# A fused scan and bilinear feed-forward kernel: one sum moved to another PSUM bank, a reciprocal and several copies, masks and scalings put in another order

## The chip, the cores and the metric

The kernel runs on one core of one Trainium2 chip. A core has five engines that follow their own instruction streams and wait for each other on semaphores: TensorE (PE, matrix products, with weight loads shown as PEld), VectorE (DVE), ScalarE (ACT), GpSimd (POOL) and SyncE (SP, which here only issues DMAs). The metric is device time in microseconds (us) for one execution, taken as the median of several runs. Before the change it is 124.18 us, with single runs of 123.66, 124.18 and 124.46 us.

## The reference

A chunked state-space scan over 4 batches, 8 heads, 768 tokens, head size 32 and state size 16 is followed by a bilinear feed-forward layer over the 3072 tokens of width 256, with an inner width of 1536.

```python
# per chunk of tokens: x (b,h,q,32), a (b,h,q), B and C (b,h,q,16)
cum = np.cumsum(log_a_chunk, axis=-1)
L = np.exp(cum[..., :, None] - cum[..., None, :]) * causal
M = np.einsum('bhin,bhjn->bhij', Cc, Bc) * L
y_intra = np.einsum('bhij,bhjd->bhid', M, xc)
y_inter = np.einsum('bhin,bhnd->bhid', Cc, state) * np.exp(cum)[..., None]
y[:, :, sl] = y_intra + y_inter
Bx = np.einsum('bhjn,bhjd->bhjnd', Bc, xc) * np.exp(cum[..., -1:] - cum)[..., None, None]
state = np.exp(log_a_chunk.sum(-1))[..., None, None] * state + Bx.sum(axis=2)
...
x = y.transpose(0, 2, 1, 3).reshape(4 * 768, 256)
return ((x @ w_a) * (x @ w_b)) @ w_out
```

## The kernel before

**Tiling.** The 768 tokens of a batch are six blocks of 128 tokens. Two batches of one block form a *pair*, so there are twelve pairs; pairs 2k and 2k+1 belong to block k. For each pair the kernel scales B and C by decay factors (`bm`, `cm`, fp16), turns them with TensorE (`transposes`), forms the products of C and B (`scores`), multiplies these by the causal mask (`mask`), and multiplies the masked products by x, adding the part that comes from the state (`pv` for pairs 0 to 3, `outputs` for whole blocks from block 2 on). The result goes into the feed-forward part.

**Feed-forward.** For pairs 0 to 3 the work is cut into *units* (`unit(p, k2)`, six to a pair): four matmuls with `Wa` into one PSUM bank (the A sum), a copy of that bank to SBUF by ACT (`evac_a`, tile `asb`, line 714), four matmuls with `Wb` into another bank (the B sum), and a product of the B sum with `asb` on DVE (`times`, tile `hk`, line 721). From block 2 on, *block units* (`bunit(blk, k)`, twelve to a block) do the same with two matmuls of 512 columns to a sum (line 768, product `hkb` at line 778). `out_half` and `bout` then multiply `hk` or `hkb` by `Wo` into a bank (`ops`), which ACT copies out and SP stores.

**PSUM.** Eight banks of 512 fp32 columns are used. Four of them are the *score banks* SC[0] to SC[3], held by two tiles of two banks each (SC0 and SC1): scores, transposes of pairs 0 to 3, state sums and outputs are written there. The other four are handed out by `bank(name)` to every A sum, B sum, `ops` sum and to some transposes. Which of the four a request gets is written out by hand: the string `BANKS` has one digit for each request in program order. A matmul that starts a sum in a bank waits until the tile that had this bank last has been read.

**Masks.** The score bank m of a pair holds four heads' products. `mask(product(p, m))` reads it on DVE, multiplies by the causal tile and writes `t1` (line 497). With `by_pool=True` ACT copies the bank to SBUF first (`tmp`, line 494), and POOL multiplies (line 495), as POOL works on SBUF here.

**Order.** The program is scheduled by hand: each engine's instructions run in the order in which the Python code emits them. `masked(p, ms, *units)` emits, turn by turn, the matmuls and the ACT copy of one unit, then one DVE mask, then the product of the unit. `go` and `bgo` emit whole units, `prep(p)` the POOL scalings of B and C of pair p (line 379, or line 191 for a block's tile `mq` that DVE turns later, line 202), `prep_x(p)` the POOL scaling of x (line 368), `loads_x(p)` a DMA from POOL's queue. `over_mid` is a reciprocal on DVE (line 282, tile `rmid`); `rmid` is read by the POOL products at lines 908 and 910, which lead to the factors G, and by `late_rows` (line 321).

**Weights.** The halves `Wa[0]`, `Wb[0]` serve units 0 to 2 of a pair, `Wa[1]`, `Wb[1]` units 3 to 5. All are loaded once, from POOL's DMA queue (line 213). Inputs of pairs 3 and up are loaded from SP's queue, whose issue starts when the first half of `Wo` has landed.

Of the kernel before, what the change touches and what calls it, by code (L numbers as in the profile page):

```python
# [19 lines left out]
YS = 16.0  # L20

BANKS = (
    "0123102031203132031023102310213021302130213021302130210312031201320132031023120310213203"
    "1203120312013021320312032130123012301231032103201320132013201320132013201320132013201320"
    "13201"
)


# [1 line left out]
def kernel(  # L30
# [18 lines left out]
    NBLK = S // Q  # L49
# [38 lines left out]
    Wa = [big.tile([128, 2, KC], f16, name=f"Wa{t}") for t in range(2)]  # L88
    Wb = [big.tile([128, 2, KC], f16, name=f"Wb{t}") for t in range(2)]
# [39 lines left out]
    SC = [SC0[:, 0], SC0[:, 1], SC1[:, 0], SC1[:, 1]]  # L129
# [8 lines left out]
    def bank(name):  # L138
        return psf.tile([128, 512], f32, name=name, tag=f"ff{next(banks)}")


    def by_block(blk, which):
        return blk >= NBLK - NT and (which == 1 or blk == NBLK - 1)
# [71 lines left out]
    def w_up(W, k, f):  # L215
        t, g = k // 6, k // 3 % 2
        return W[t][:, f, g * 384 : (g + 1) * 384].rearrange("p (c kk) -> p kk c", kk=3)[:, k % 3]
# [63 lines left out]
    def over_mid(lo, hi):  # L281
        nc.vector.reciprocal(rmid[:, lo:hi], Pr[:, lo:hi, 63])
# [154 lines left out]
    def scores(p):  # L437
        BT, CT = st[p]["BT"], st[p]["CT"]
        st[p]["T1"] = mid.tile([128, H, 2, Q], f16, name="t1", tag="t1")
        for e, bt, m in itertools.product(range(2), range(2), range(4)) if p >= P0 else ():  # L440
            rows = slice(32 * m, 32 * m + 32)
            c0 = (e * 2 + bt) * Q
            nc.tensor.matmul(  # L443
                SC[m][:, c0 : c0 + Q],
                BT[rows, e, bt],
                CT[rows, bt],
                start=True,
                stop=True,
                skip_group_check=True,
                tile_position=(32 * m, 0),  # L450
            )
        for e in range(2) if p < P0 else ():
            for r in range(2):
                for m in range(4):
                    for bt in range(2):
                        rows = slice(32 * m, 32 * m + 32)
                        c0 = (e * 2 + r) * Q
                        nc.tensor.matmul(  # L458
                            SC[m][64 * bt : 64 * bt + 64, c0 : c0 + Q],
                            BT[rows, e, r, bt],  # L460
                            CT[rows, bt],
                            start=True,
                            stop=True,
                            skip_group_check=True,
                            tile_position=(32 * m, 64 * bt),
                        )

    def product(p, m):

        if p >= P0:  # L470
            return (
                st[p]["T1"][:, 2 * m : 2 * m + 2].rearrange("p e t q -> p (e t) q"),
                SC[m].rearrange("p (c q) -> p c q", q=Q),
                causal_q.unsqueeze(1).broadcast_to((128, 4, Q)),
            )
        return (
            st[p]["T1"][:, 2 * m : 2 * m + 2].rearrange("p e r q -> p e (r q)"),
            SC[m].rearrange("p (e c) -> p e c", e=2),
            causal.rearrange("p r q -> p (r q)").unsqueeze(1).broadcast_to((128, 2, 2 * Q)),
        )  # L480
# [9 lines left out]
    def mask(out_in, by_pool=False):  # L490
        o_, i_, c_ = out_in
        if by_pool:
            tmp = mid.tile([128, *c_.shape[1:]], f32, name="tmp", tag="tmp")
            nc.scalar.copy(tmp, i_)  # L494
            nc.gpsimd.tensor_tensor(out=o_, in0=tmp, in1=c_, op=ALU.mult)  # L495
        else:
            nc.vector.tensor_tensor(out=o_, in0=i_, in1=c_, op=ALU.mult)  # L497
# [184 lines left out]
            )  # L682
        st.setdefault(("S", p + NBP), {})["Sbd"] = Sbd

    def unit_mm(p, k2, W):
        ps = bank("aps" if W is Wa else "bps")
        for kk in range(2):
            k = 2 * k2 + kk
            for f in range(2):
                nc.tensor.matmul(  # L690
                    ps[:, kk * 2 * Q : (kk + 1) * 2 * Q],
                    w_up(W, k, f),
                    X2T[:, p, :, f],
                    start=(f == 0),
                    stop=(f == 1),
                    skip_group_check=True,
                )
        return ps
# [13 lines left out]
    def evac_a(a_ps, on_dve=False):  # L712
        asb = ffh.tile([128, 512], f32, name="asb", tag="asb", bufs=5)
        (nc.vector.tensor_copy if on_dve else nc.scalar.copy)(asb, a_ps)  # L714
        return asb

    def times(p, k2, b_ps, asb):
        s = st[p]
        if "hk" not in s:
            s["hk"] = ffh.tile([128, NK, 2 * Q], f16, name="hk", tag="hk")  # L720
        nc.vector.tensor_tensor(  # L721
            out=s["hk"][:, 2 * k2 : 2 * k2 + 2, :].rearrange("p k q -> p (k q)"), in0=b_ps, in1=asb, op=ALU.mult
        )

    def unit(p, k2, between=None):
        a_ps = unit_mm(p, k2, Wa)
        asb = evac_a(a_ps)
        if between:
            between()
        b_ps = unit_mm(p, k2, Wb)  # L730
        return lambda: times(p, k2, b_ps, asb)

    def out_mm(p, bt, o_ps, ks):
        hk = st[p]["hk"]
        for k in ks:
            nc.tensor.matmul(  # L736
                o_ps[:, 0:d_model],
                hk[:, k, bt * Q : (bt + 1) * Q],
                Wo[:, k, :],
                start=(k == 0),  # L740
                stop=(k == NK - 1),
                skip_group_check=True,
            )

    def out_store(p, bt, o_ps):
        blk, bp = divmod(p, NBP)
        o_sb = outp.tile([128, d_model], f32, name="osb", tag="osb")
        nc.scalar.activation(out=o_sb, in_=o_ps[:, 0:d_model], func=AF.Copy, scale=1.0 / (YS * YS))
        r0 = (2 * bp + bt) * S + blk * Q
        stores.append(lambda: nc.sync.dma_start(out[r0 : r0 + Q, :], o_sb))  # L750
        if p > 1:
            store_all()

    def out_half(p, bt):
        o_ps = bank("ops")
        out_mm(p, bt, o_ps, range(NK))
        out_store(p, bt, o_ps)
# [22 lines left out]
    def bgo(blk, *ks):  # L780
        for k in ks:
            bunit(blk, k)()
# [48 lines left out]
    def go(*items):  # L831
        for p, k2 in items:
            unit(p, k2)()
# [49 lines left out]
    aps = [bank("aps") for _ in range(3)]  # L883
# [15 lines left out]
    bps = [bank("bps") for _ in range(3)]  # L899
# [3 lines left out]
    units_mm(0, range(3), Wb, bps, 0, range(4, 6))  # L903
    units_mm(0, range(3), Wb, bps, 1, range(2, 6))
    nc.scalar.copy(maskbd, headm.unsqueeze(2).broadcast_to((128, H, D)))
    times(0, 0, bps[0], asb[0])
    over_mid(2, NBLK)
    nc.gpsimd.tensor_tensor(out=hr, in0=Pr[:, 0:NG, Q - 1], in1=rmid[:, 0:NG], op=ALU.mult)
    nc.gpsimd.tensor_tensor(out=hs, in0=hr, in1=Pr[:, 1:NBLK, 63], op=ALU.mult)
    nc.gpsimd.tensor_tensor(  # L910
# [10 lines left out]
    scale_bc(2, 0, nc.gpsimd)  # L921
    scale_bc(2, 1, nc.gpsimd)
    load_wo(1)
    go((1, 0), (1, 1))
    late_rows(nc.vector)
    rows = store_rows(nc.sync)
    go((1, 2))
# [15 lines left out]
    aps = [unit_mm(0, 3, Wa), unit_mm(0, 4, Wa)]  # L943
# [11 lines left out]
    h = unit(1, 4)  # L955
# [5 lines left out]
    h = unit(1, 5)  # L961
# [17 lines left out]
    h = unit(2, 0, lambda: transposes(3, apart=True))  # L979
    h()  # L980
    h = unit(2, 1)

    def prep(p, spread=()):
        if p < NP:
            for w in (1, 0):
                if not by_block(p // NBP, w):
                    scale_bc(p, w, nc.gpsimd)
                elif p % NBP == 0:
                    scale_block(p // NBP, w, nc.gpsimd)
        for q in spread:  # L990
            if q // NBP < NBLK - 1:
                state_spread(q)

    def prep_x(p):
        if p < NP:
            scale_x(p, nc.gpsimd)
# [17 lines left out]
    def masked(p, ms, *units):  # L1014
        for i in range(max(len(ms), len(units))):
            h = units[i]() if i < len(units) else None
            if i < len(ms):
                mask(product(p, ms[i]))
            if h:
                h()  # L1020

    def pu(p, *ks):
        return [lambda k=k: unit(p, k) for k in ks]

    def bu(blk, *ks):
        return [lambda k=k: bunit(blk, k) for k in ks]
# [26 lines left out]
    prep_x(4)  # L1053

    scores(4)
    mask(product(4, 3), by_pool=True)
    prep_x(5)
    prep(6)
    masked(4, (0, 1))
    masked(4, (2,), *pu(3, 0))  # L1060
    go((3, 1), (3, 2))
    scores(5)
    mask(product(5, 3), by_pool=True)
    out_half(2, 1)
    prep(7)
    h = unit(3, 3)
    mask(product(5, 0))
# [2 lines left out]
    h = unit(3, 4)  # L1070
# [22 lines left out]
    for p in range(9, NP):  # L1093
        loads_x(p)
    prep(10)
    masked(7, (0, 1, 2), *bu(2, 5, 6, 7, 8, 9, 10, 11))
    turn_pair(8, 1)
    group(3)
    transposes(8)
# [81 lines left out]
```

## Time and profile before

| | us |
|---|---|
| median of the runs | 124.18 |
| lowest and highest run | 123.66, 124.46 |
| the profiled execution's own time | 123.89 |
| its span (first to last instruction) | 122.2 |
| TensorE busy | 116.0 |
| VectorE busy | 92.8 |
| ScalarE busy | 76.6 |
| GpSimd busy | 65.6 |

The times inside the profile are counted from the start of the span. A row of the timeline gives the start, the busy time, the engine, the line of the kernel, the operation, the written and read tiles, the shapes and how many instructions in a row are merged into it; in brackets stands the idle time of the engine ahead of it, and who ended the idle time. Matmuls are pipelined: a row of four matmuls is shown as 0.60 us long, although the next four start 0.44 us after it. For TensorE the distance between starts is therefore the thing to read, and not the busy time. Instructions of DVE and ACT overlap in the same way by some hundredths of a microsecond.

### The profile page before, as it was taken

What the parts mean: (1) busy time and instruction counts of PE and PEld (TensorE: products, weight loads), DVE (VectorE), ACT (ScalarE), POOL (GpSimd) and SP (SyncE); (2) the same over time, 40 slices, a digit from 0 to 9 for tenths busy, and PEclk for the clock granted to TensorE, in tenths of its full rate; (3) what the DMA queues carried; (4) which work ended last, traced back from release to release, by engine and by line L of the source; (5) the groups of instructions that cost most, each with busy time, mean ns of one, the idle gap of its engine ahead of it and who ended that gap; (6) DMA issues with size and microseconds to landing.
All of it is one profiled execution on the core that took longest, in us unless ns stands there. A gap on an engine that the chain in (4) does not pass through costs nothing.

```text
span 122.2 us, 3719 instructions
## 1 busy us (share of the span) xinstructions
PE 116.0 (95%) x1440; PEld 79.1 (65%) x1440; DVE 92.8 (76%) x183; ACT 76.6 (63%) x157; POOL 65.6 (54%) x92
## 2 busy tenths in 40 slices
PE   6789799999999999999999999999999999999990
PEld 2245589889898798744467464766464775555890
DVE  4999789895886979699995999996898444847200
ACT  0447856837669855987659757666757736557220
POOL 7987997599892995083999379319034000000000
PEclk9999999999999999999999999999999999999999
DMA  3999979997996288169636991011101012010132
GB/s 67 181 161 213 207 160 218 133 179 76 110 124 117 43 82 130 37 80 126 121 73 135 253 348 60 0 48 46 43 0 43 5 43 86 0 43 5 41 88 86
DMA packets 46017, 12.25 MB, mean 100 GB/s; under 512 B 40000, under 2 KB 45568, under 8 KB 46000
## 3 DMA queue, kind: packets, MB, share of 16 engines
q1 hardware_dynamic: 41344, 7.62, 32.6%
q0 software_dynamic: 2384, 3.98, 17.2%
q10 hardware_dynamic: 2272, 0.43, 1.8%
q8 instruction: 11, 0.18, 0.6%
q14 instruction: 6, 0.05, 0.1%
HBM read 11.18 MB, written 3.19 MB: 118 GB/s over the span
## 4 chain that ended last, share of the span: by engine, by line
PE 85%; DMA 6%; POOL 4%; ACT 1%; DVE 1%; issue 1%
PE ops L793 18%; PE aps L768 17%; PE bps L768 16%; PE ops L736 9%; PE aps L690 8%; PE bps L690 7%; DMA Wb<-in_moe_w_b_dram 6%; PE SC L443 2%; PE SC L503 2%; PE bps L703 1%; POOL bn L165 1%; POOL cn L165 1%; ACT asb L714 1%; PE tr L409 1%; PE SC L518 1%; PE SC L593 1%
## 5 line engine op out<-in xcount | busy, mean ns | idle before, releaser
L714 ACT COPY asb<-aps 128x512 f32<-128x512 f32 x72 | 42.0, 589 | 14.4 <-PE aps L768 9.3
L778 DVE TENSOR_TENSOR hkb<-bps,asb 128x512 f16<-128x512 f32 x48 | 32.0, 687 | 10.5 <-ACT asb L714 9.9
L768 PE MATMUL aps<-XB,Wa 128*128 128x512 f16 x96 | 28.6, 379 | 0.1
L768 PE MATMUL bps<-XB,Wb 128*128 128x512 f16 x96 | 28.5, 379 | 0.0
L793 PE MATMUL ops<-Wo,hkb 128*128 128x256 f16 (+1 forms) x204 | 22.6, 267 | 0.0
L793 PEld LDWEIGHTS <-hkb 128*128 128x128 f16 x204 | 18.5, 98 | 3.0
L721 DVE TENSOR_TENSOR hk<-bps,asb 128x512 f16<-128x512 f32 x24 | 15.9, 683 | 3.0 <-ACT asb L714 2.1
L497 DVE TENSOR_TENSOR t<-SC,causal_q 128x512 f16<-128x512 f32 x24 | 15.5, 682 | 3.2 <-PE SC L443 3.2
L495 POOL TENSOR_TENSOR t<-tmp,causal_q 128x512 f16<-128x512 f32 x8 | 9.3, 1158 | 14.5 <-ACT tmp L494 14.3
L768 PEld LDWEIGHTS <-Wb 128*128 128x128 f16 x96 | 9.9, 103 | 10.9
L768 PEld LDWEIGHTS <-Wa 128*128 128x128 f16 x96 | 9.7, 103 | 9.2 <-issue 0.3
L368 POOL TENSOR_SCALAR x<-xn 128x512 f16<-128x512 f32 x8 | 11.9, 1492 | 3.0 <-DMA xn<-in_x_dram 2.4
L805 ACT ACTIVATE osb<-ops 128x256 f32<-128x256 f32 (+1 forms) x16 | 6.0, 378 | 11.2 <-PE ops L793 11.2
L690 PE MATMUL aps<-X2T,Wa 128*128 128x256 f16 x84 | 12.5, 273 | 0.3 <-ACT asb L714 0.2
L690 PE MATMUL bps<-X2T,Wb 128*128 128x256 f16 x84 | 12.4, 272 | 0.0
L736 PE MATMUL ops<-Wo,hk 128*128 128x256 f16 x96 | 11.6, 273 | 0.0
L736 PEld LDWEIGHTS <-hk 128*128 128x128 f16 x96 | 9.0, 98 | 1.2
L690 PEld LDWEIGHTS <-Wa 128*128 128x128 f16 x84 | 8.3, 104 | 1.3 <-issue 0.6
L690 PEld LDWEIGHTS <-Wb 128*128 128x128 f16 x84 | 8.6, 103 | 0.5
L497 DVE TENSOR_TENSOR t<-SC,causal 128x512 f16<-128x512 f32 x13 | 8.2, 682 | 0.9 <-PE SC L458 0.8
L494 ACT COPY tmp<-SC 128x512 f32<-128x512 f32 x11 | 6.6, 596 | 1.9 <-PE SC L443 1.1
L202 DVE STREAM_TRANSPOSE tq<-mq 128x256 f16<-128x256 f16 x8 | 5.9, 742 | 0.0
(111 smaller groups left out, 136.9 us busy)
## 6 DMA issues: line engine op xcount, KB each, us to landing
out_dram<-osb SPq DMA_DIRECT2D x17, 128.0 KB, 3.2
xn<-in_x_dram SPq DMA_DIRECT2D x5, 256.0 KB, 4.6
out_dram<-osb SPq DMA_DIRECT2D x13, 64.0 KB, 1.5
Wo<-in_moe_w_out_dram POOLq DMA_DIRECT2D x2, 384.0 KB, 5.0
bn<-in_B_dram SPq DMA_DIRECT2D x6, 128.0 KB, 4.0
rq<-in_C_dram SPq DMA_DIRECT2D x24, 32.0 KB, 2.2
xn<-in_x_dram POOLq DMA_DIRECT2D x3, 256.0 KB, 5.0
xn<-in_x_dram SPq DMA_DIRECT2D x4, 128.0 KB, 5.4
```

What stands on the lines that cost most here:

```text
L368: eng.tensor_scalar(xo, xi, XS, None, ALU.mult)
L494: nc.scalar.copy(tmp, i_)
L495: nc.gpsimd.tensor_tensor(out=o_, in0=tmp, in1=c_, op=ALU.mult)
L497: nc.vector.tensor_tensor(out=o_, in0=i_, in1=c_, op=ALU.mult)
L690: nc.tensor.matmul(ps[:, kk * 2 * Q : (kk + 1) * 2 * Q], w_up(W, k, f), X2T[:, p, :, f], start=(f == 0), stop=(f == 1), skip_group_check=True,
L714: (nc.vector.tensor_copy if on_dve else nc.scalar.copy)(asb, a_ps)
L721: nc.vector.tensor_tensor(out=s["hk"][:, 2 * k2 : 2 * k2 + 2, :].rearrange("p k q -> p (k q)"), in0=b_ps, in1=asb, op=ALU.mult)
L736: nc.tensor.matmul(o_ps[:, 0:d_model], hk[:, k, bt * Q : (bt + 1) * Q], Wo[:, k, :], start=(k == 0), stop=(k == NK - 1), skip_group_check= ...
L768: nc.tensor.matmul(t_, w_up(W, k, f), XB[:, blk - P0 // NBP, f].rearrange("p t j q -> p (t j q)"), start=(f == 0), stop=(f == 1), skip_gro ...
L778: return lambda: nc.vector.tensor_tensor(out=s["hk"][:, k], in0=ps[1], in1=asb, op=ALU.mult)
L793: nc.tensor.matmul(o_ps[:, 0:w], hk[:, k, c * Q : (c + 1) * Q], Wo[:, k, cs], start=(k == 0), stop=(k == NK - 1), skip_group_check=True,)
L805: nc.scalar.activation(out=o_sb[:, 0:w], in_=o_ps[:, 0:w], func=AF.Copy, scale=1.0 / (YS * YS))
```

## The change

One string is written anew, and the order of some instructions is changed. No instruction is added or removed, and TensorE's own order stays as it was.

- `over_mid(2, NBLK)` is emitted ahead of the first product of unit (0,0), and not behind it.
- The A sum of unit (1,1) goes into the score bank SC[0] instead of one of the four rotating banks. `BANKS` has one digit less, and its digits behind that place are assigned anew.
- Pairs 4 and 5: the x of pair 5 is scaled by POOL ahead of the POOL mask of pair 4 instead of behind it. The ACT copy for this mask is emitted behind ACT's copy of the A sum of unit (3,0) instead of ahead of it. The DVE mask of bank 2 of pair 4 comes behind the product of unit (3,0) instead of ahead of it. `prep(6)`, the scalings of pair 6 with the C of block 3, moves from ahead of these masks to behind the POOL mask of pair 5.
- Pair 7: its DVE mask of bank 2 moves by one unit, from the turn of block unit 7 into that of block unit 8.

```diff
 BANKS = (
-    "0123102031203132031023102310213021302130213021302130210312031201320132031023120310213203"
-    "1203120312013021320312032130123012301231032103201320132013201320132013201320132013201320"
-    "13201"
+    "0123102031203123012301230123102310231023102310231023102130213012301230210321302103123021"
+    "0321032103123012032103201231023102310213201320312031203120312031203120312031203120312031"
+    "2031"
 )
...
-    def unit_mm(p, k2, W):
-        ps = bank("aps" if W is Wa else "bps")
+    def unit_mm(p, k2, W, ps=None):
+        if ps is None:
+            ps = bank("aps" if W is Wa else "bps")
...
-    def unit(p, k2, between=None):
-        a_ps = unit_mm(p, k2, Wa)
+    def unit(p, k2, between=None, ps=(None, None)):
+        a_ps = unit_mm(p, k2, Wa, ps[0])
         asb = evac_a(a_ps)
         if between:
             between()
-        b_ps = unit_mm(p, k2, Wb)
+        b_ps = unit_mm(p, k2, Wb, ps[1])
         return lambda: times(p, k2, b_ps, asb)
...
+    over_mid(2, NBLK)
     times(0, 0, bps[0], asb[0])
-    over_mid(2, NBLK)
...
-    go((1, 0), (1, 1))
+    go((1, 0))
+    unit(1, 1, ps=(SC[0], None))()
     late_rows(nc.vector)
...
     scores(4)
+    prep_x(5)
+    masked(4, (0, 1))
+    h = unit(3, 0)
     mask(product(4, 3), by_pool=True)
-    prep_x(5)
-    prep(6)
-    masked(4, (0, 1))
-    masked(4, (2,), *pu(3, 0))
+    h()
+    mask(product(4, 2))
     go((3, 1), (3, 2))
     scores(5)
     mask(product(5, 3), by_pool=True)
     out_half(2, 1)
+    prep(6)
     prep(7)
...
     prep(10)
-    masked(7, (0, 1, 2), *bu(2, 5, 6, 7, 8, 9, 10, 11))
+    masked(7, (0, 1), *bu(2, 5, 6))
+    bgo(2, 7)
+    masked(7, (2,), *bu(2, 8, 9, 10, 11))
```

## The prediction, made before the changed kernel was run

> **What bounds the kernel now.** I read the page's busy shares and its chain of work first, then TensorE's timeline for places where the distance between starts is longer than elsewhere, and at each such place the timelines of ACT, DVE and POOL.
>
> ```profile
> PE 116.0 (95%) x1440; PEld 79.1 (65%) x1440; DVE 92.8 (76%) x183; ACT 76.6 (63%) x157; POOL 65.6 (54%) x92
> PE 85%; DMA 6%; POOL 4%; ACT 1%; DVE 1%; issue 1%
> ```
>
> TensorE is busy for 95% of the span, and 85% of the chain that ended last is TensorE's. The rest of the chain is the load of the first weights at the start. From then on the end moves only by what TensorE gains or loses between two of its own instructions, and a gap that closes is worth its length unless a later instruction then waits. Three such gaps lie where the change acts.
>
> ```profile
> 14.90 0.60 PE L690 MATMUL aps<-X2T,Wa 128*128 128x256 f16 x4
> 15.34 0.60 PE L690 MATMUL bps<-X2T,Wb 128*128 128x256 f16 x4
> 16.17 0.60 PE L690 MATMUL aps<-X2T,Wa 128*128 128x256 f16 x4 [0.24 <-ACT asb L714]
> ...
> 40.71 0.60 PE L690 MATMUL bps<-X2T,Wb 128*128 128x256 f16 x4
> 41.33 0.60 PE L690 MATMUL aps<-X2T,Wa 128*128 128x256 f16 x4
> 41.82 0.60 PE L690 MATMUL bps<-X2T,Wb 128*128 128x256 f16 x4
> 42.34 0.40 PE L443 MATMUL SC<-ct,bt 32*128 32x128 f16 x16
> ...
> 59.66 0.59 PE L768 MATMUL bps<-XB,Wb 128*128 128x512 f16 x2
> 60.32 0.59 PE L768 MATMUL aps<-XB,Wa 128*128 128x512 f16 x2
> ```
>
> A sum of four matmuls is followed after 0.44 us (14.90 to 15.34); two wide ones stream as many columns. Against that, the A sum of unit (1,1) comes 0.83 after its forerunner (15.34 to 16.17): 0.39 lost. The sums of unit (3,2) come after 0.62 and 0.49: 0.18 and 0.05, together 0.23 lost. The A sum of block unit (2,10) comes after 0.66: 0.22 lost. In all 0.84 us, the most that the change can gain here.
>
> **The change part by part.**
>
> *The A sum of unit (1,1) in SC[0].*
>
> ```profile
> 15.54 0.59 ACT L714 COPY asb<-aps 128x512 f32<-128x512 f32 x1 [0.47 <-PE aps L690]
> 16.80 0.59 ACT L714 COPY asb<-aps 128x512 f32<-128x512 f32 x1 [0.68 <-PE aps L690]
> 17.91 0.30 PE L929 MATMUL SC<-hsx,c 128*128 128x20 f32 x2
> ...
> 19.27 1.04 PE L690 MATMUL bps<-X2T,Wb 128*128 128x256 f16 x8
> ...
> L213 POOL DMA_DIRECT2D Wb<-in_moe_w_b_dram x3: 594/602/728, 6.2 to 9.8; - x3
> DMA to landing us min/median/max: 6.8/7.2/9.1
> ```
>
> By the old string this sum has the bank of unit (1,0)'s A sum, which ACT reads until 16.13 (15.54 + 0.59); the matmul starts 0.04 later. SC[0] has lain idle since the masks of pair 1, so the sum starts at 15.78 and the 0.39 go. ACT's copy starts 0.63 after the sum (16.17 to 16.80), so at 16.41, and is done at 17.00. The next writer of SC[0] is the small product at 17.91, which moves to 17.52: half a microsecond of room.
>
> What is late next is a load. The B sums of units (0,3) and (0,4) at 19.27 would start at 18.88, and they are the first to read the second half of Wb. That is the last of its three loads, issued at 9.8 with the longest way, 9.1 us: it lands at 18.9. This queue hears nothing of TensorE. With both figures rounded to 0.1 the loss lies between 0 and 0.1; I take 0.05, so this part gains 0.34.
>
> The Trainium skill, in "DMA: Bandwidth & Descriptors", section "Anatomy of one DMA — SWDGE (gpsimd) path", puts a load from GpSimd at about 2.0 us plus its bytes over 436 GB/s, which for 384 KB is an estimate of 2.9 us. By it the half would be there at 12.7 and this part would gain 0.39. The row's 9.1 us is three times that, and so I go by the row.
>
> *The reciprocal ahead of the product.*
>
> ```profile
> 14.52 0.69 DVE L721 TENSOR_TENSOR hk<-bps,asb 128x512 f16<-128x512 f32 x1 [0.67 <-PE bps L703]
> 15.12 0.16 DVE L282 RECIPROCAL rmid<-Pr 32x4 f32<-32x4 f32 x1
> 15.21 1.84 DVE L721 TENSOR_TENSOR hk<-bps,asb 128x512 f16<-128x512 f32 x3
> ...
> 15.63 0.24 POOL L908 TENSOR_TENSOR hr<-Pr,rmid 32x5 f32<-32x5 f32 x1
> ```
>
> DVE idles 0.67 ahead of the product at 14.52; the 0.16 fit in. The next three products come 0.09 earlier (15.21 against 15.12) and free their banks that much earlier. POOL reads `rmid` at 15.63, and that row has no idle time ahead of it: POOL came from other work, so it gains nothing. I cost this at nothing by itself. Without that idle time it would delay the first product by 0.16.
>
> *Pairs 4 and 5.*
>
> ```profile
> 40.17 0.62 ACT L494 COPY tmp<-SC 128x512 f32<-128x512 f32 x1
> 40.65 1.11 ACT L714 COPY asb<-aps 128x512 f32<-128x512 f32 x2
> ...
> 39.48 2.03 DVE L497 TENSOR_TENSOR t<-SC,causal_q 128x512 f16<-128x512 f32 x3 [0.78 <-PE SC L443]
> 41.43 1.28 DVE L721 TENSOR_TENSOR hk<-bps,asb 128x512 f16<-128x512 f32 x2
> ...
> 39.63 1.49 POOL L368 TENSOR_SCALAR x<-xn 128x512 f16<-128x512 f32 x1
> 41.20 1.17 POOL L495 TENSOR_TENSOR t<-tmp,causal_q 128x512 f16<-128x512 f32 x1
> 42.45 1.49 POOL L368 TENSOR_SCALAR x<-xn 128x512 f16<-128x512 f32 x1
> 44.02 1.10 POOL L191 TENSOR_TENSOR mq<-rq,fCq 128x512 f16<-128x512 f32 x1
> 45.08 0.62 POOL L379 TENSOR_TENSOR bm<-bn,fBl 128x256 f16<-128x256 f32 x1
> 45.66 1.16 POOL L495 TENSOR_TENSOR t<-tmp,causal_q 128x512 f16<-128x512 f32 x1
> ...
> 46.96 0.63 PE L503 MATMUL SC<-t,x 128*32 128x128 f16 x32
> ...
> 47.64 0.29 PE L409 MATMUL tr<-ident,bm 128*128 128x128 f16 x2
> ```
>
> Times here are those of before; the whole stage comes 0.34 earlier. Unit (3,2)'s A sum has the bank of unit (3,0)'s, whose copy starts only at 40.65, behind the mask copy `tmp`. Now the two change places: the copy of (3,0) runs from 40.17 to 40.79, and the A sum can start at its natural 41.15 (40.71 + 0.44). The mask copy follows until about 41.3. The new string gives the B sum of (3,2), due at 41.59, the bank of (3,0)'s B sum. Its product starts when `asb` is there, at 40.83, where DVE's third mask stood, and ends near 41.5: just in time. The third mask now runs from 41.43 to 42.11. The scores of pair 5, due at 42.11 (42.34 less 0.23), write the bank that it reads. A semaphore's way is the 0.04 seen above, so they lose about 0.05. This part gains 0.18; its bounds are 0.1 and 0.23.
>
> On POOL, x of pair 5 takes the place of the mask (41.20; the next instruction starts 1.57 later, as from 39.63 to 41.20), the two masks follow at 42.8 and 43.9, then `mq` at 45.0 and `bm` of pair 6 from 46.1 to 46.7. TensorE turns that `bm` at 47.64, which becomes 47.46: 0.75 of room, where there were 1.9. The mask of pair 5 ended at 46.82, just ahead of the products at 46.96, and now ends at 45.0. No DMA is among the moved steps.
>
> *Pair 7.*
>
> ```profile
> 58.99 0.68 DVE L497 TENSOR_TENSOR t<-SC,causal_q 128x512 f16<-128x512 f32 x1
> 59.59 1.87 DVE L778 TENSOR_TENSOR hkb<-bps,asb 128x512 f16<-128x512 f32 x3
> ```
>
> The A sum of unit 10 has the bank of unit 7's B sum, whose product stands behind the mask and ends at 60.27. With the mask one place later the product runs from 58.99 to 59.67, and the sum can start at 60.10. The mask and the product of unit 8 then stand where they stood. Unit 9's product ends at 61.46 as before, too late for unit 11's B sum, now due at 61.42 (three sums on), which had its bank; the new string gives it unit 10's A bank, free at 61.36 (60.10 + 0.63 + 0.59, and the semaphore's 0.04). Gain 0.22, with 0.15 as its lower bound, should one of these tight places miss.
>
> Sum: 0.34 + 0.18 + 0.22 = 0.74. Comparing who had each bank last under the two strings, I find eight requests with another forerunner, all in these three places; everywhere else the digits are only renamed.
>
> The profiled execution took 123.89 with a span of 122.2, so 1.7 lie outside. It becomes 121.5 and 123.15. Its time is 0.29 below the median of the three runs; from the median the sum gives 124.18 - 0.74 = 123.4, my forecast.
>
> **The rivals.**
>
> *Inputs that do not move give part of it back.* What TensorE gains, loads from the queues do not.
>
> ```profile
> 65.18 0.91 SPq L183 DMA_DIRECT2D rq<-in_B_dram  x2
> ...
> DMA to landing us min/median/max: 3.0/3.1/4.4
> ...
> 70.93 1.10 POOL L191 TENSOR_TENSOR mq<-rq,fBq 128x512 f16<-128x512 f32 x1 [2.60 <-DVE tq L202]
> 76.23 1.16 POOL L495 TENSOR_TENSOR t<-tmp,causal_q 128x512 f16<-128x512 f32 x1
> 77.15 0.63 PE L503 MATMUL SC<-t,x 128*32 128x128 f16 x32
> ```
>
> The last issue of block 5's B starts at about 65.7; of the last issues the slowest took 4.4 us, which would land it at 70.1. POOL takes it at 70.93 after a wait for DVE, which becomes 70.19: 0.1 of room. From there POOL has no pause until its mask ends at 77.39, which the end of the row at 77.15 reads. A load that is 0.4 later costs 0.3. With the Wb half 0.1 late, the gain is 0.4: 123.8. Chance 0.22.
>
> *Nothing arrives.* The gaps close, and TensorE waits the same time at the next bank: unit (0,3)'s B sum, scores of pair 5, unit 11. The rooms counted there are 0.05 or less, which speaks for some loss, but the waits of three places would all have to return in full: 124.2. Chance 0.05.
>
> *Slower: POOL becomes the bound at pair 6.* All POOL work between 41.20 and `bm` of pair 6 now stands ahead of TensorE's 47.46. If POOL's instructions stretch because they lie beside other DVE work than before, 5.5 us (41.20 to 46.7) have to grow by more than the room of 0.75 and the gain of 0.74, that is by over 1.5, to end slower. Grown by half, 2.75, they cost 2.0 at pair 6, a net loss of 1.26: 125.4. Against it: the POOL scalings of x at 39.63 and 42.45 both took 1.49 beside different DVE instructions, and the masks 1.17 and 1.16. Chance 0.04, with 0.02 for other slow ends. The Trainium skill, in "GPSIMD Engine Reference", section "1. Specifications", says that GpSimd shares its SBUF interfaces with VectorE and contends with DVE instructions that have two SBUF inputs or run in a two-port mode. By that rule the stretch could happen; DVE's masks and products here read one operand from PSUM, and the equal POOL rows show no stretch.
>
> **How the numbers follow.** The forecast has 0.67. The range goes from 122.7 (the fastest run of before, 123.66, less the full 0.84, and 0.1 for a faster draw) to 124.2 (the first two rivals). Within 1% means 122.94 to 125.42, about what a measurement of this kernel can tell from no change. The sum of 0.74 is 0.6%, and no gap is left that would make it 1.24; only the spread of the runs can, for which I give 0.10. Slower by over 1% is the POOL rival, 0.05. Same: 0.85.
>
> **What would show it.** In the profile of the changed kernel, the A sum of unit (1,1) starts 0.44 after its forerunner; the B sums of (0,3) start at 18.9 and name the Wb load if anything; unit (3,2) is 0.44 behind (3,1), and the scores of pair 5 start at 41.8; unit 10 of block 2 follows within 0.45, and the span is near 121.5. The prediction is wrong if TensorE waits for `bm` at pair 6, for POOL's mask of pair 9, or at a bank outside the three places.

## The result, and the profile after

The changed kernel takes 123.14 us (median of 22 runs, 122.61 to 124.46); the kernel before, run beside it, takes 123.92 (median of 22, 123.38 to 124.82). The ratio is 0.994, with a 95% interval from 0.9917 to 0.9964. It is faster by 0.6%, 0.74 us of 123.92, and by 0.4 to 1.0 us within the interval; the two medians differ by 0.78. The ratio leaves out one slow run of the changed kernel, the 124.46. The forecast was a gain of 0.74 and 123.4 us; it started from the three runs' median of 124.18, which is 0.26 above the one here.

The first lines of the page of the changed kernel, and its chain of waits:

```profile
PE 116.0 (96%) x1440; PEld 79.5 (66%) x1440; DVE 92.8 (77%) x183; ACT 76.6 (63%) x157; POOL 65.8 (54%) x92
...
PE 87%; DMA 5%; POOL 4%; issue 0%; ACT 0%; DVE 0%
```

No engine does less than before. TensorE's 116.0 us now fill 96% of a span of 121.2, and ACT and DVE have all but gone from the chain. Before, ACT stood in it at the gap of unit (1,1) and ACT and DVE at that of block unit 10; at unit (3,2) the chain named TensorE alone, so that there only the distance between starts shows the gap. TensorE's timeline at the three places:

```profile
14.69 0.60 PE L691 MATMUL aps<-X2T,Wa 128*128 128x256 f16 x4
15.13 0.60 PE L691 MATMUL bps<-X2T,Wb 128*128 128x256 f16 x4
15.56 0.60 PE L691 MATMUL SC<-X2T,Wa 128*128 128x256 f16 x4
17.31 0.30 PE L931 MATMUL SC<-hsx,c 128*128 128x20 f32 x2
18.67 1.04 PE L691 MATMUL bps<-X2T,Wb 128*128 128x256 f16 x8
...
40.10 0.60 PE L691 MATMUL bps<-X2T,Wb 128*128 128x256 f16 x4
40.54 0.60 PE L691 MATMUL aps<-X2T,Wa 128*128 128x256 f16 x4
40.98 0.60 PE L691 MATMUL bps<-X2T,Wb 128*128 128x256 f16 x4
41.51 0.45 PE L443 MATMUL SC<-ct,bt 32*128 32x128 f16 x16
41.89 0.72 PE L737 MATMUL ops<-Wo,hk 128*128 128x256 f16 x5
...
58.87 0.59 PE L769 MATMUL bps<-XB,Wb 128*128 128x512 f16 x2
59.30 0.59 PE L769 MATMUL aps<-XB,Wa 128*128 128x512 f16 x2
```

All three gaps are shut: each sum follows its forerunner by 0.43 to 0.44. The rows of ACT and DVE that free the banks, at the same places (ACT's first, then DVE's):

```profile
16.20 0.59 ACT L715 COPY asb<-SC 128x512 f32<-128x512 f32 x1 [0.29 <-PE SC L691]
...
39.57 0.62 ACT L715 COPY asb<-aps 128x512 f32<-128x512 f32 x1
40.05 0.63 ACT L494 COPY tmp<-SC 128x512 f32<-128x512 f32 x1
```

```profile
40.22 0.69 DVE L722 TENSOR_TENSOR hk<-bps,asb 128x512 f16<-128x512 f32 x1
40.83 0.68 DVE L497 TENSOR_TENSOR t<-SC,causal_q 128x512 f16<-128x512 f32 x1
...
57.61 1.28 DVE L779 TENSOR_TENSOR hkb<-bps,asb 128x512 f16<-128x512 f32 x2
58.80 0.68 DVE L497 TENSOR_TENSOR t<-SC,causal_q 128x512 f16<-128x512 f32 x1
```

The copy of SC[0] ends at 16.79, ahead of the small product at 17.31. The copy of unit (3,0)'s A sum ends at 40.19 and the product of its B sum at 40.91; the sums that take these two banks start at 40.54 and 40.98. The second product of the row at 57.61 is that of unit 7; it ends at 58.89, and unit 10's A sum starts at 59.30.

Where the time went is read by laying both traces side by side, matmul by matmul, and noting where their distance changes. Unit (1,0) starts at 14.69 instead of 14.90; these 0.21 come from the first of Wb's three loads, which landed at 12.82 in this execution and at 13.03 in the one before, and not from the change. The distance grows by 0.40 at unit (1,1), by 0.23 at unit (3,2), shrinks by 0.03 over the scores of pair 5, and grows by 0.22 at block unit 10. Nothing else changes it for good by more than 0.03 us. The change is thus worth 0.81 in this execution, and the luck of that load 0.21.

For the experiments I therefore use the *stretch*: from unit (1,0)'s first matmul to the start of the last matmul. It leaves out the loads at the start. It is 104.23 us before and 103.43 after.

### The profile page after: what moved, and what is told of

Its sections match the earlier page's. It is cut to its first block, busy times and chain, and to the rows that moved or that the text cites. A ratio compares the mean times of both kernels' runs of the same rounds, so it can differ in the third digit from the quotient of the medians.

```text
span 121.2 us, 3718 instructions
## 1 busy us (share of the span) xinstructions
PE 116.0 (96%) x1440; PEld 79.5 (66%) x1440; DVE 92.8 (77%) x183; ACT 76.6 (63%) x157; POOL 65.8 (54%) x92
## 4 chain that ended last, share of the span: by engine, by line
PE 87%; DMA 5%; POOL 4%; issue 0%; ACT 0%; DVE 0%
PE ops L794 18%; PE aps L769 17%; PE bps L769 17%; PE ops L737 9%; PE aps L691 8%; PE bps L691 8%; DMA Wb<-in_moe_w_b_dram 5%; PE SC L443 2%; PE SC L503 2%; PE bps L704 1%; POOL bn L165 1%; POOL cn L165 1%; PE tr L409 1%; PE SC L518 1%; POOL Wa L213 1%; PE SC L593 1%
## 5 line engine op out<-in xcount | busy, mean ns | idle before, releaser
L691 PE MATMUL aps<-X2T,Wa 128*128 128x256 f16 x80 | 11.9, 274 | 0.0
L267 PE MATMUL SC<-warm 128*128 128x512 f16 (+1 forms) x14 | 5.2, 530 | 1.0 <-POOL warm L238 1.0
```

The source lines that it names most:

```text
L691: nc.tensor.matmul(ps[:, kk * 2 * Q : (kk + 1) * 2 * Q], w_up(W, k, f), X2T[:, p, :, f], start=(f == 0), stop=(f == 1), skip_group_check=True,
```

## The experiments

**The scatter of the stretch.** The kernel before, unedited.

> The kernel before, once more, to see the scatter of the measure that the next runs use: the stretch from the first matmul of unit (1,0)'s A sum to the start of the last matmul, which leaves out the loads at the start. It was 104.23 us before and 103.43 after the change. If TensorE's own waits make the difference (my theory), the stretch of this run is within 0.05 of 104.23. If it is scatter of loads and queues, it is off by some tenths.

The stretch was 104.23 again, 0.003 us off, although unit (1,0) started at 14.65 instead of 14.90. The scatter of these two traces lies ahead of unit (1,0); what TensorE does behind it repeats to some nanoseconds. A difference of a few hundredths of a microsecond in one trace can be read, once a wait for a late load is taken out.

**Unit (1,1) alone.** The kernel before with one edit; its string lacks the digit of unit (1,1)'s A sum and is otherwise kept.

```diff
-    go((1, 0), (1, 1))
+    go((1, 0))
+    unit(1, 1, ps=(SC[0], None))()
```

> Only the A sum of unit (1,1) in SC[0]; the old string with that one digit taken out, so that the only other request with a new forerunner is the B sum of unit (1,2). Theory: the stretch from unit (1,0) to the end falls by 0.39 to 103.84; if the second half of Wb lands later than TensorE asks for it, by less, 0.3 to 0.39, and the B sum of unit (0,3) waits for the load. The gaps of 0.23 at unit (3,2) and 0.22 at block unit (2,10) stay. Rival, the wait comes back at the next bank: stretch within 0.1 of 104.23.

The gain at unit (1,1) is 0.40. The second half of Wb cost nothing. But the stretch fell by only 0.04, to 104.20, as 0.36 were lost again at a place that neither theory had. TensorE's timeline there, then POOL's, of this kernel:

```profile
28.70 0.27 PE L409 MATMUL SC<-ident,bm 128*128 128x128 f16 x2
29.16 0.29 PE L409 MATMUL SC<-ident,cm 128*128 128x128 f16 x2 [0.19 <-POOL cm L379]
```

```profile
26.13 0.62 POOL L379 TENSOR_TENSOR bm<-bn,fB 128x256 f16<-128x256 f32 x1
28.48 0.62 POOL L379 TENSOR_TENSOR cm<-cn,fC 128x256 f16<-128x256 f32 x1 [1.74 <-DMA cn<-in_C_dram]
```

TensorE turns pair 3's B and wants to turn its C 0.11 later. POOL scales that C only at 28.48, having waited 1.74 us for its load. In the changed kernel's trace POOL scaled it at 27.69 and TensorE did not wait:

```profile
27.08 0.62 POOL L379 TENSOR_TENSOR bm<-bn,fB 128x256 f16<-128x256 f32 x1 [0.74 <-DMA bn<-in_B_dram]
27.69 0.62 POOL L379 TENSOR_TENSOR cm<-cn,fC 128x256 f16<-128x256 f32 x1
```

**Order without the string.** The new order at pairs 4 to 7 in the kernel before, with the old digits.

```diff
     scores(4)
-    mask(product(4, 3), by_pool=True)
     prep_x(5)
-    prep(6)
     masked(4, (0, 1))
-    masked(4, (2,), *pu(3, 0))
+    h = unit(3, 0)
+    mask(product(4, 3), by_pool=True)
+    h()
+    mask(product(4, 2))
...
     out_half(2, 1)
+    prep(6)
     prep(7)
...
-    masked(7, (0, 1, 2), *bu(2, 5, 6, 7, 8, 9, 10, 11))
+    masked(7, (0, 1), *bu(2, 5, 6))
+    bgo(2, 7)
+    masked(7, (2,), *bu(2, 8, 9, 10, 11))
```

> The new order of copies, masks and scalings (pairs 4 to 7) with the old string, and nothing at unit (1,1). Theory: the order alone frees the bank of unit (3,2)'s A sum, 0.18 earlier, but its B sum then waits for the bank of unit (3,1)'s A sum, whose copy ends where it ended, so the gain there is 0 (0 to 0.05); at block unit 10 the 0.22 are gained and about 0.1 lost again at unit 11's B sum, whose bank unit 9's product frees late. Stretch 104.23 - 0.12 = 104.1. Rival, the order does it and the digits are only names: stretch 104.23 - 0.41 = 103.8.

The stretch was 104.13, a gain of 0.11, as reckoned. TensorE's timeline of this kernel:

```profile
40.61 0.60 PE L690 MATMUL bps<-X2T,Wb 128*128 128x256 f16 x4
41.05 0.60 PE L690 MATMUL aps<-X2T,Wa 128*128 128x256 f16 x4
41.71 0.60 PE L690 MATMUL bps<-X2T,Wb 128*128 128x256 f16 x4
...
60.42 0.59 PE L768 MATMUL bps<-XB,Wb 128*128 128x512 f16 x2
60.85 0.59 PE L768 MATMUL aps<-XB,Wa 128*128 128x512 f16 x2
61.41 0.59 PE L768 MATMUL bps<-XB,Wb 128*128 128x512 f16 x2
```

The A sum of unit (3,2) comes in time (40.61 to 41.05), and its B sum is late instead (41.05 to 41.71): the gap has moved by one request. Unit 11's B sum is late by 0.13 (60.85 to 61.41). The order alone gains 0.11, order and digits together 0.41. The new digits without any of the new order were not run.

**GpSimd's order alone.** The changed kernel with this edit:

```diff
-    prep_x(5)
     masked(4, (0, 1))
     h = unit(3, 0)
     mask(product(4, 3), by_pool=True)
+    prep_x(5)
+    prep(6)
     h()
...
     out_half(2, 1)
-    prep(6)
     prep(7)
```

> The changed kernel with GpSimd's instructions at pairs 4 to 6 in the old order: mask of pair 4, x of pair 5, the scalings of pair 6, then the mask of pair 5. Theory: that mask ends about 0.1 ahead of the products that read it, so the stretch stays at 103.43, at most 0.1 more. Rival, the new GpSimd order is what pays at pairs 4 and 5: the stretch is longer by 0.2 or more, and TensorE waits at the outputs of block 2.

The stretch was 103.89, 0.46 longer, and all of it lies at the matmuls that turn pair 3's C, 12 us ahead of the edit. From there on this kernel and the changed one run in step, through pairs 4 to 6 too. The new place of x(5) and `prep(6)` is worth nothing here.

**The changed kernel again.**

> The changed kernel once more. Two looks with the A sum of unit (1,1) in SC[0] showed TensorE waiting 0.36 and 0.46 us at the turn of pair 3's C, whose load came late, and the first half of Wo, which releases pair 3's loads, landed at 22.2 to 22.8 in three of three such looks, against 21.4 to 21.6 in three looks without that part. Theory, the earlier stages of this kernel meet loads that do not move: the half of Wo lands at 22.2 or later again, and the stretch is 103.43 or up to 0.5 longer, all of it at the turn of pair 3. Rival, chance: Wo lands at 21.4 to 21.6, and the stretch is 103.43.

Pair 3's C came late again, by 0.34, and the stretch was 103.77. The ratio was 0.995 (0.993 to 0.997).

**Pair 3's loads without their rule.** In the changed kernel one line is taken out.

```diff
-    tc.add_manual_dep(b3[0].ins, wo0.ins.name, AFTER, reason="weights ahead of pair 3's inputs")
```

> The changed kernel without the rule that pair 3's loads wait for the first half of Wo. Theory, these loads are what is next: they are issued at 18 to 19 instead of 22.2, pair 3's C is there well ahead of its turn, the stretch is 103.43 in every look, and the time is at or below the changed kernel's by 0 to 0.3. Rival, the loads then share the DMA engines with Wo: a half of Wo lands after 24 or 27, TensorE waits at the output products, and the stretch is 103.7 or more.

Here the rival held in the main. The loads were issued at 18.2, the wait at pair 3 was gone, and TensorE waited for the second half of Wo in its stead. TensorE's timeline:

```profile
26.76 1.47 PE L737 MATMUL ops<-Wo,hk 128*128 128x256 f16 x12 [0.48 <-DMA Wo<-in_moe_w_out_dram]
```

The stretch was 103.97 and the ratio 0.9967 (0.9943 to 0.9991), no better than the changed kernel. The landings were not quite those of the rival: the first half of Wo came at 21.4, as early as in any trace with the rule, and the second at 26.72, which is 0.2 behind the latest with the rule (26.50). That Wo was late because it shared the DMA engines with these loads is thus likely, and not shown. This half has little room with the rule, too: in three of the twelve traces of the table below it landed only 0.1 to 0.2 ahead of its first matmul.

**VectorE's mask ahead of the product again,** in the changed kernel:

```diff
-    h()
     mask(product(4, 2))
+    h()
```

> The changed kernel with VectorE's mask of bank 2 of pair 4 ahead of the product of unit (3,0) again, and the new string and all other orders kept. Theory: VectorE may read that bank pair only when ScalarE's copy of the other half is done (40.68 in the changed kernel's trace), so the mask runs from 40.7 to 41.4, the product until 42.0, and the B sum of unit (3,2), which has its bank, starts at 42.05 instead of 40.98: the stretch is 103.43 + 1.07 = 104.5, less a little that is regained later. Rival, VectorE's order does not matter there: stretch within 0.1 of 103.43. (A wait of pair 3's C of up to 0.5 is to be taken out of either.)

The stretch was 104.73, of which 0.28 are pair 3's wait. The edit costs 1.07 at the B sum of unit (3,2) and nothing is regained but some hundredths over the scores. VectorE's timeline, then TensorE's, of this kernel:

```profile
38.91 1.29 DVE L497 TENSOR_TENSOR t<-SC,causal_q 128x512 f16<-128x512 f32 x2 [0.78 <-PE SC L443]
40.73 0.69 DVE L497 TENSOR_TENSOR t<-SC,causal_q 128x512 f16<-128x512 f32 x1 [0.54 <-ACT tmp L494]
41.34 1.28 DVE L722 TENSOR_TENSOR hk<-bps,asb 128x512 f16<-128x512 f32 x2
```

```profile
40.57 0.60 PE L691 MATMUL aps<-X2T,Wa 128*128 128x256 f16 x4
42.08 0.60 PE L691 MATMUL bps<-X2T,Wb 128*128 128x256 f16 x4 [0.91 <-DVE hk L722]
```

The mask is held until ACT's copy of the other bank of its pair is done, and the product behind it holds the bank that TensorE wants. So the new digits and ScalarE's new order lose without VectorE's. ScalarE's new order was not tried by itself.

**The reciprocal back behind the product,** in the changed kernel:

```diff
-    over_mid(2, NBLK)
     times(0, 0, bps[0], asb[0])
+    over_mid(2, NBLK)
```

> The changed kernel with the reciprocal back behind the first product. Theory: nothing waits for it, the three products behind it come 0.09 later and their banks have more room than that, so the stretch is 103.43 within 0.05 (a wait of pair 3's C of up to 0.5 taken out). Rival, one of the banks around unit (1,1) was freed just in time: 0.05 to 0.16 longer.

The stretch was 103.43, with no wait at pair 3. The reciprocal's place is worth nothing that can be seen.

**The row store later,** in the changed kernel:

```diff
+    go((1, 2))
     late_rows(nc.vector)
     rows = store_rows(nc.sync)
-    go((1, 2))
```

> The changed kernel with unit (1,2) ahead of the factor rows and their store, so that the store is issued near 18.7 as in the kernel before, and not near 18.0. In six looks with the A sum of unit (1,1) in SC[0] the first half of Wo landed at 22.2 to 22.8 and TensorE waited 0 to 0.46 at the turn of pair 3's C; in three without it, at 21.4 to 21.6 with no wait. Theory, the earlier store gets in the way of Wo: it lands at 21.4 to 21.6 again, no wait at pair 3, stretch 103.43. Rival, the store has nothing to do with it: Wo lands at 22.2 or later, stretch up to 103.9.

Neither came out whole. The first half of Wo was as late as in the other traces with unit (1,1) in SC[0] (pair 3's loads, released by it, were issued at 22.5), so the store is not what delays it; yet there was no wait, and the stretch was 103.43. The ratio was 0.9932 (0.9908 to 0.9955).

**Pairs 4 to 7 without unit (1,1).** The edit of "order without the string", with digits that give the requests there the forerunners that they have under the new string; unit (1,1) as before.

> The new order at pairs 4 to 7 with the banks that it needs, and unit (1,1) as before. Theory: 0.19 and 0.22 are gained, the stretch is 103.82, pair 3's loads are in time because TensorE comes to them 0.4 later, and the time is 0.3% below the kernel before. That is 0.1 to 0.2 us short of the changed kernel's time, as pair 3's wait takes back about half of what unit (1,1) gains there. Rival, pair 3's C is late here as well: stretch 104.0 or more.

Without pair 3's wait of 0.33 the stretch of 104.15 is 103.82, as forecast. But that wait was there. Counted from unit (1,0), TensorE comes to pair 3's C 0.39 later than in the changed kernel (14.75 against 14.36); but unit (1,0) itself began at 14.36 in this trace and at 14.69 in that of the changed kernel, so that the turn was due at 29.11 in the one and at 29.05 in the other. The loads can be late for either kernel, and an early unit (1,0) leaves them less time. The ratio was 0.9949 (0.9927 to 0.9972).

**Both once more, side by side.**

> The changed kernel on the same chip and beside the same runs of the kernel before as the next one. By the looks so far its stretch is 103.43 when pair 3's C is in time and up to 103.9 when not, and its time 0.994 to 0.995 of the kernel before.

> The changed kernel with unit (1,2) ahead of the factor rows and their store, again, beside the changed kernel. Its one look had no wait at pair 3 although Wo landed at 22.5, and its ratio was 0.9932 against 0.995 in another call. Theory, that was luck of the loads: the two ratios of this call differ by less than 0.002, and a wait at pair 3 of 0 to 0.5 shows in either. Rival, the order is better: its ratio is lower by 0.002 or more and it does not wait at pair 3.

The changed kernel had 0.9948 (0.9923 to 0.9974) and a stretch of 103.73 with a wait of 0.29 at pair 3. The other order had 0.9958 (0.9925 to 0.9992), so it is no better. Its profiled execution took 129.49 us, against 122.80 to 124.35 for its other runs, and is left out below.

The other traces with pair 3's loads under their rule (us; "ready" is the end of POOL's scaling of pair 3's C, "due" is when TensorE would turn it without a wait; a matmul starts about 0.06 behind "ready"):

| kernel | unit (1,1) in SC[0] | pair 3's loads issued from | C ready | turn due | TensorE's wait | stretch | stretch less wait |
|---|---|---|---|---|---|---|---|
| before | no | 21.66 | 28.10 | 29.65 | 0 | 104.23 | 104.23 |
| before, again | no | 21.50 | 27.85 | 29.40 | 0 | 104.23 | 104.23 |
| order, old digits | no | 21.44 | 27.99 | 29.55 | 0 | 104.13 | 104.13 |
| pairs 4 to 7 alone | no | 22.35 | 29.38 | 29.11 | 0.33 | 104.15 | 103.82 |
| after | yes | 22.23 | 28.31 | 29.05 | 0 | 103.43 | 103.43 |
| after, again | yes | 22.40 | 29.38 | 29.10 | 0.34 | 103.77 | 103.43 |
| after, third | yes | 22.57 | 29.13 | 28.89 | 0.29 | 103.73 | 103.43 |
| unit (1,1) alone | yes | 22.82 | 29.10 | 28.81 | 0.35 | 104.20 | 103.85 |
| GpSimd's old order | yes | 22.62 | 29.25 | 28.84 | 0.46 | 103.89 | 103.43 |
| mask first | yes | 22.71 | 29.02 | 28.80 | 0.28 | 104.73 | 104.45 |
| reciprocal back | yes | 22.30 | 28.56 | 28.71 | 0 | 103.43 | 103.43 |
| row store later | yes | 22.48 | 28.76 | 28.95 | 0 | 103.43 | 103.43 |

## Why the prediction was right, step by step

**TensorE bounds, and a gap is worth its length.** Right. Taken without pair 3's wait, the parts add up to within 0.01: 0.39 for unit (1,1) alone (104.23 - 103.85, rounded) and 0.41 for pairs 4 to 7 alone make 0.80, and both together give 0.81.

**Unit (1,1).** The mechanism and the 0.39 were right. The term for the second half of Wb was mis-sized: I took 0.05 from the one landing at 18.9, and the sums that need it never waited. The changed kernel's rows for that load:

```profile
L213 POOL DMA_DIRECT2D Wb<-in_moe_w_b_dram x3: 591/602/731, 6.2 to 9.4; - x3
...
DMA to landing us min/median/max: 6.6/7.0/8.4
```

It was there at 17.8 (9.4 + 8.4), and was asked for at 18.67. The 18.9 of the profile before was a late landing: in the other eleven traces of the table it came at 17.55 to 18.11. The Trainium skill's sum in "DMA: Bandwidth & Descriptors", section "Anatomy of one DMA — SWDGE (gpsimd) path", an estimate of 2.9 us, gave the right answer, no wait, with a duration a third of the measured one.

**Pairs 4 and 5.** Right to 0.01. The scores of pair 5 did take longer: they start 0.38 ahead of the next sum (41.51 to 41.89) instead of 0.34 (42.34 to 42.68). That is the wait for the third mask that I had put at 0.05: the mask ends at 41.51 (40.83 + 0.68), and the third of these matmuls, the first to write its bank, starts at 41.56. The gain left is 0.19; I said 0.18. On POOL the order was as reckoned and, as one run showed, indifferent. What the prediction did not say is how sharp the order on VectorE is: mask and product exchanged cost 1.07.

**Pair 7.** 0.22 forecast, 0.22 measured; with the old digits 0.13 of it are lost at unit 11, where I had reckoned 0.1.

**The reciprocal.** Nothing forecast, nothing found. Of the two POOL products named ahead, only the one at line 908 reads `rmid` itself; the one at line 910 works on its result.

**The rivals.** "Inputs that do not move give part of it back" is what happens, at another place than I said: the rival's loss was 0.3, and the waits in six of the twelve traces of the table are 0.28 to 0.46. I had named the second half of Wb and block 5's B. In the changed kernel POOL took block 5's B at 69.91 after a wait of 2.9 for VectorE, as before, and no trace shows TensorE waiting there:

```profile
69.91 1.10 POOL L191 TENSOR_TENSOR mq<-rq,fBq 128x512 f16<-128x512 f32 x1 [2.93 <-DVE tq L202]
```

The room of 0.1 there was that of one execution: the last of these loads landed at 70.04 in the trace before, and at 64.8 to 68.8 in the seven others that hold the landings of all eight, 1.0 us or more ahead of POOL's taking it. The place is pair 3's C, which I never looked at, since in the profile before it was ready 1.5 us early (28.10 for a turn at 29.65); no sign that the prediction named for its being wrong covers it. In the table it was ready at 28.3 to 29.4 in the eight traces with unit (1,1) in SC[0], and at 27.8 to 28.1 in three of the four without. The earlier turn alone would bring no wait: a C that is ready by 28.1 is in time for the earliest turn of the table, 28.71. The mean wait is 0.22 in the eight and 0.08 in the four. From 0.81 this leaves 0.67, which the measured 0.4 to 1.0 holds as well as the forecast's 0.74. My sum came out close because its two errors were small and opposed: no loss at Wb, and a loss at pair 3. That the measured ratio gives 0.74 to the hundredth is luck, as the interval is 0.6 wide. "Nothing arrives" and "POOL becomes the bound" have no support in any run.

**What stays open.** Why the first half of Wo lands between 21.4 and 22.8, and with it pair 3's loads. It was early in three of the four traces without the change at unit (1,1) and late in all eight with it, but one without was late too, and one with it and without the rule was early (21.4). The row store was tried and is not the cause.

## What to carry to other kernels

Where one engine sets the end, compare the distances between its starts with the shortest that the same instructions have elsewhere; what is over is the whole gain to be had, and it can be priced row by row. Buffers dealt out by hand and the order of their readers are one thing: here the new order with the old digits only moved a gap by one request, and the new digits with one reader in its old place cost more than they gain. Before booking a gain early in a kernel, list every load that a later stage waits for, with the room that it has in several executions and not in one: a load need not come earlier because its user does, and the two loads that one profile showed as tight here were not, while one that it showed as early was.

## What the runs showed of the hardware that was not expected

TensorE's own course repeats to nanoseconds. The stretch was 104.234 and 104.231 in the two traces of the kernel before, and 103.427, 103.425 and 103.426 in three traces of kernels with the change and no wait at pair 3. Behind unit (1,0), all the scatter in the table lies in one landing: the load of pair 3's C made TensorE wait 0 or 0.28 to 0.46. Ahead of it, unit (1,0) started anywhere from 14.35 to 14.90, and the first of Wb's three loads landed from 12.17 to 13.03; in the main the two go together.
